# Two more feature blocks of an FFN as block products, another group of features first behind attention, and V of the last chunk computed later

## The chip, the cores and the metric

The kernel runs on one core of a Trainium2 chip. The metric is the device time of one execution in microseconds, the median of several runs. All times below are of single executions or of such medians.

## The reference, cut to what matters

x has 2048 rows of width 640. The result mixes, row by row with a gate, a causal attention with a compressive memory (32 heads of width 20, four chunks of 512 rows) and a gated feed-forward network (FFN) with 1728 features:

```python
g = sigmoid((x * gate_w).sum(-1, keepdims=True))
# attention: q, k, v = x @ wq, x @ wk, x @ wv; for each chunk s of 4:
    logits = q_s @ k_s.T * scale + mask;  a_dot = softmax(logits) @ v_s
    num = phi(q_s) @ M;  den = phi(q_s) @ z + 1e-6;  a_mem = num / den
    o_s = gb * a_mem + (1 - gb) * a_dot        # gb = sigmoid(beta), one per head
    M, z = M + phi(k_s).T @ v_s, z + phi(k_s).sum()
a = o @ wo
# FFN
b = (silu(x @ w1) * (x @ w3)) @ w2
out = g * a + (1 - g) * b
```

All products are of float32 accuracy: both factors are split into a high and a low part, and a product is made of three passes (high x high, high x low, low x high).

## The kernel before, in words

**Tiles.** x comes transposed, five tiles of 128 x 512 for each chunk of 512 rows (`X`, high and low). The 1728 features are 13 blocks of 128 (0 to 12) and half a block of 64, which is called 13. The chunks go in two pairs, A = (0, 1) and B = (2, 3). A feature block of one chunk is made by `ffn_up`: `proj` for the gate (`g`, 15 products of 512 columns: five tiles, three passes) and for the up projection (`u`, 15 products); then ACT and DVE make silu times up and split it into `ht` (high by a cast on ACT, low by a subtraction on POOL). `ffn_down` multiplies a group of three blocks with five column blocks of w2 and adds the result to `acc`: for a group with `lead`, feature block by feature block into five banks at once (30 products for two blocks of features, 45 for three); otherwise column block by column block.

**Block products.** `ffn_unit` makes a feature block pair (gate and up of one feature block, for both chunks of a pair) in another way: `unit` works with seven products of sums of blocks (named a, w, x, y here; a is `f_ff` in the trace), with sums of X that `build_sums` makes once for a pair, and sums of weights that `w_split` makes for each unit on DVE. In pair B, `build_sums(B)` needs the buffers that attention holds, so units of B stand behind attention.

**Weights.** Each weight tile of 128 x 640 is loaded into one of two raw buffers (`wr`, `NRAW`), split by a cast and a subtraction on POOL (L223, L228) into one of six tiles `W` (`NW`), and used by TensorE in order. `w_step` at each step of the dense work loads and splits ahead; `w_get` forces it.

**Attention.** Heads go in quads, 32 quads in all, forty slots each. Two visits a quad: a long one at slot 5 (`s` of the quad, `t` and `o` of the ones before) and a short one at slot 17 (the rest of `s`, and one `t`). `s` are the logits for the row maxima (DVE), `max_rows` turns the maxima and writes them by two small DMAs on ACT's queue into two rows of the tile `qk`; `t` then gives the transposed logits less the maximum, ACT the exponential `P`, `o` the product with v. `load_pair` loads q and k of two heads from DRAM into `qk` by two DMAs.

**What sets the order.** TensorE's order is the program's own (written by hand): a `head`, then attention's slots with dense work between them, then a `tail`. The dense work of attention is a list of segments `segs`, each with the slot at which it has to be done and a list of jobs; a credit in us hands it out evenly over the slots of the segment. `braid(a, b, every, at=...)` puts steps of b between the steps of a. The other engines' order comes from a scheduler, which sorts the instructions by a modelled time; `here` and `behind` pin some of them. `GROUPS` says which feature blocks make one down projection; `LATE` is one such group.

**The places of the change.** Before, GROUPS of B are [0,1,2], [3,4,5], [6,7,8], [9,10,13] (LATE), [11,12]. V of chunks 2 and 3 is computed in the second segment one behind the other (`job_v(B)`), with one loading of the five V weights; features 0 and 1 of B stand in the third. Chunk 3's V isn't kept in SBUF for the memory; its parts go through `ht` buffers (six, `NHT`) and are stored to DRAM. The gate's exponent comes out of V's products, and `gate_turn(3)` transposes it, in K's first block. The tail is half block 13, the loads of the gate's shares, the down projection of [9,10,13] with the sums of X between its steps, unit 11 with the first part of the output projection of chunk 3 between, the output projection, unit 12, and the last down projection.

## Time and profile before

| | |
|---|---|
| median of three runs | 1089.4 us (1089.33 to 1090.75) |
| profiled execution, its own time | 1089.61 us |
| its span in the profile | 1087.9 us |
| TensorE (PE) | 1080.8 us busy, 99%, 6230 products |
| weight loads of TensorE (PEld) | 841.9 us, 77% |
| VectorE (DVE) | 706.9 us, 65% |
| GpSimd (POOL) | 612.8 us, 56% |
| ScalarE (ACT) | 407.0 us, 37% |
| granted TensorE clock | 1.0 of full speed |

A row of a group gives line, engine, operation, output and inputs without their numbers, shapes and a count; after the bar the busy us, the mean ns of one, and the idle us of the engine just before, with what ended most of it. A row of a timeline gives start us, duration us, engine, line and operation, and in brackets what the engine waited for. "f32" products of 512 columns here have overlapping durations, so a price comes from the distance of starts, not from durations. POOLq and ACTq are the queues on which those engines issue DMAs. Lines are those of the kernel before; in the changed kernel they are a few higher.

### The profile page before, as it was taken

Reading aid. Unit: us, or ns where it says so; the run is one execution under the profiler, and the core shown is the slowest. Engines: PE = TensorE matmul, PEld = TensorE weight load, DVE = VectorE, ACT = ScalarE, POOL = GpSimd, SP = SyncE. Lnnn points to the kernel's source line nnn. Section 1 sums busy time; section 2 is a strip of 40 time slices with the busy share of each in tenths; the row PEclk is TensorE's granted clock in tenths of the full one; section 3 lists DMA queues with packets and bytes.
Section 4 is the critical chain, followed back from the end, with each engine's and each line's share of the span. In section 5 each row is a group of like instructions: output and inputs, shape, how many; then the busy total and the mean of one; then the engine's idle time right before and its main releaser. Section 6 shows DMA issues by size and latency. Waiting matters only on the chain.

```text
span 1087.9 us, 18072 instructions
## 1 busy us (share of the span) xinstructions
PE 1080.8 (99%) x6230; PEld 841.9 (77%) x6230; DVE 706.9 (65%) x1867; ACT 407.0 (37%) x874; POOL 612.8 (56%) x751
## 2 busy tenths in 40 slices
PE   9999999999999999999999999999999999999998
PEld 7988878777777777778977777777777777777787
DVE  6477782756765658785344678875557775554996
ACT  6355322233332432245354543424333332242321
POOL 3089674646563664475366447655674664656382
PEclk9999999999999999999999999999999999999999
DMA  9557420553543554555377966455654433435212
GB/s 330 195 179 267 166 61 25 122 111 106 144 114 79 132 135 120 149 155 162 112 242 247 297 218 182 102 159 144 157 143 112 114 102 97 108 93 171 78 47 110
DMA packets 89450, 157.39 MB, mean 145 GB/s; under 512 B 11888, under 2 KB 26128, under 8 KB 89360
## 3 DMA queue, kind: packets, MB, share of 16 engines
q1 hardware_dynamic: 63904, 106.76, 30.8%
q0 software_dynamic: 21424, 42.42, 17.0%
q10 hardware_dynamic: 4032, 7.08, 1.9%
q8 instruction: 49, 0.80, 0.3%
q14 instruction: 41, 0.34, 0.1%
HBM read 100.76 MB, written 54.54 MB: 143 GB/s over the span
## 4 chain that ended last, share of the span: by engine, by line
PE 97%; DMA 1%; ACT 1%; DVE 1%; issue 0%; SPq 0%; DVEq 0%; ACTq 0%
PE f L868 15%; PE g L319 14%; PE u L319 13%; PE v L450 7%; PE op L1125 7%; PE o L970 7%; PE s L914 5%; PE t L949 4%; PE q L319 3%; PE k L319 3%; PE f L854 2%; PE x_ff L554 2%; PE y_ff L554 2%; PE f_ff L554 2%; PE nd L417 2%; PE pm L710 1%
## 5 line engine op out<-in xcount | busy, mean ns | idle before, releaser
L921 DVE CUSTOM_DVE_ANT_0 junk<-s,mask 128x256 bf16<-128x256 f32 (+3 forms) x512 | 249.9, 488 | 86.1 <-PE s L914 53.9
L955 ACT ACTIVATE P<-t 128x512 f32<-128x512 f32 (+1 forms) x384 | 172.0, 538 | 166.8 <-PE t L949 117.3
L228 POOL TENSOR_TENSOR W<-wr,W 128x640 fp32r<-128x640 f32 (+2 forms) x118 | 187.0, 1589 | 19.1 <-ACT W L223 16.8
L960 POOL TENSOR_SCALAR_AFFINE_SELECT P<-P 128x256 f32<-128x256 f32 x192 | 93.6, 497 | 181.0 <-ACT P L955 180.8
L868 PE MATMUL f<-ht,W 128*128 128x512 f32 (+1 forms) x689 | 165.6, 396 | 0.3 <-ACT P L955 0.3
L319 PE MATMUL g<-X,W 128*128 128x512 f32 x660 | 165.0, 398 | 0.3 <-ACT P L955 0.3
L319 PE MATMUL u<-X,W 128*128 128x512 f32 x600 | 152.6, 400 | 0.0
L223 POOL CAST W<-wr 128x640 fp32r<-128x640 f32 (+2 forms) x114 | 86.7, 765 | 116.4 <-PE v L450 34.0
L868 PEld LDWEIGHTS f<-ht,W 128*128 128x128 f32 x689 | 127.4, 188 | 31.1 <-ACT P L955 0.5
L319 PEld LDWEIGHTS g<-X,W 128*128 128x128 f32 x660 | 122.3, 188 | 29.1 <-issue 0.4
L319 PEld LDWEIGHTS u<-X,W 128*128 128x128 f32 x600 | 110.2, 188 | 26.9 <-issue 0.6
L118 POOL TENSOR_TENSOR ht<-ft,ht 128x512 fp32r<-128x512 f32 x40 | 52.1, 1302 | 79.7 <-ACT ht L117 79.5
L891 POOL DMA_DIRECT2D qk<-qkd x128 | 83.4, 653 | 0.3 <-PE s L914 0.2
L914 PE MATMUL s<-qk 60*128 60x256 f32 (+3 forms) x512 | 78.4, 347 | 0.2 <-DVE oq L974 0.2
L970 PE MATMUL o<-P,vg 128*32 128x512 f32 (+3 forms) x1024 | 75.5, 435 | 0.0
L450 PE MATMUL v<-W,X 128*128 128x320 f32 (+1 forms) x480 | 72.4, 311 | 0.0
L450 PEld LDWEIGHTS v<-W,X 128*128 128x128 f32 x480 | 71.2, 189 | 0.8 <-DVE X L145 0.3
L914 PEld LDWEIGHTS s<-qk 60*128 60x128 f32 x512 | 46.6, 185 | 24.2 <-issue 18.5
L970 PEld LDWEIGHTS o<-P,vg 128*32 128x32 f32 x1024 | 30.4, 109 | 41.3 <-issue 31.8
L949 PE MATMUL t<-qk 62*128 62x256 f32 (+3 forms) x512 | 61.8, 320 | 0.4 <-ACT ft L795 0.3
L837 DVE TENSOR_TENSOR acc<-f,acc 128x512 f32<-128x512 f32 x65 | 44.1, 686 | 21.0 <-PE f L868 20.7
L949 PEld LDWEIGHTS t<-qk 62*128 62x128 f32 x512 | 46.2, 186 | 13.0 <-issue 6.9
(310 smaller groups left out, 1604.0 us busy)
## 6 DMA issues: line engine op xcount, KB each, us to landing
qk<-qkd POOLq DMA_DIRECT2D x128, 240.0 KB, 4.1
wr<-in_w_dram SPq DMA_DIRECT2D x69, 320.0 KB
qkd<-qs SPq DMA_DIRECT2D x20, 512.0 KB
qkd<-ks SPq DMA_DIRECT2D x20, 512.0 KB
od<-oq SPq DMA_DIRECT2D x32, 256.0 KB
wr<-in_wo_dram SPq DMA_DIRECT2D x20, 320.0 KB
vg<-vd SPq DMA_DIRECT2D x16, 336.0 KB
xr<-in_xT_dram SPq DMA_DIRECT2D x20, 256.0 KB
```

The source lines that it names most:

```text
L223: hi = (nc.scalar.copy if act else nc.gpsimd.tensor_copy)(w[:, 0, :n], src)
L228: last["low"] = nc.gpsimd.tensor_sub(w[:, 1, :n], src, w[:, 0, :n].bitcast(F32))
L319: nc.tensor.matmul(ps, w[:, a, kb * P:(kb + 1) * P], x[:, b, kb, :], start=n == 0, stop=n == 14)
L450: nc.tensor.matmul(ps[:, :n1 - n0], x[:, a, kb, lb * P:(lb + 1) * P], wvt[kb][:, b, n0:n1], start=n == 0, stop=n == 14)
L868: nc.tensor.matmul(ps[:, :n1 - n0], w, h, start=n == 0, stop=n == len(ms) - 1)
L891: here(nc.gpsimd.dma_start(t[64 * i:64 * i + RH], qkd[c][RH * (h + i):RH * (h + i + 1)]))
L914: nc.tensor.matmul(ps[i][:, o:o + w], q[:, qb * P:(qb + 1) * P], key[:, :w], start=n == 0, stop=n == len(todo) - 1, skip_group_check=True)
L921: r = nc.vector.tensor_tensor_reduce(out=junk[:, :w], in0=ps[i][:, o:o + w], in1=mask[:, L - w:], scale=1.0, scalar=-3.0e38, op0=ALU.add, ...
L949: nc.tensor.matmul(ps[i][:, o:o + L - kb * P], key[:, kb * P:(kb + 1) * P], q[:, kb * P:], start=n == 0, stop=n == len(todo) - 1, skip_gro ...
L955: last["exp"] = nc.scalar.activation(pairs[2 * m + k]["P"][:, i, o:o + n], ps[i][:, b:b + n], AF.Exp, scale=SCALE)
L960: nc.gpsimd.affine_select(d, d, pattern=[[0, 2], [0, n], [1, P]], base=0, channel_multiplier=-1, compare_op=ALU.is_ge, fill=0.0)
L970: nc.tensor.matmul(ps[32 * i:32 * i + 32, kb * P:], heads[2 * p + i]["v"][:, kb], pairs[p + i // 2]["P"][:, i % 2, o:o + n], start=kb == 0 ...
```

## The change

Pair B's groups become [0,1,2], [3,4,5], [6,7,8] (LATE), [13,9,10], [11,12]. Blocks 9 and 10 of B are made by `ffn_unit`, in the tail, as 11 and 12 are. The tail opens with the down projection of [6,7,8], with the sums of X between its steps; then the loads of the shares, half block 13, unit 9 with the first part of the output projection, the output projection, unit 10, the down projection of [13,9,10], units 11 and 12, and the last down projection. V of chunk 3 is moved to the end of the third segment, behind features 0 and 1 of B; for that the V weights are loaded and split a second time. The split of chunk 3's X goes between V of chunk 2 (`XV`), `gate_turn(3)` into feature 2 (`last_gate`). Block 5 of B moves to the fifth segment. The ends of three segments, counted in heads of ten slots, are later by 0.5 (`E2`), 4 (`E3`) and 1 (`E4`). The steps between which the output projections' first parts stand are other ones (`O0A`, `O1A`, `O2A`), as are those of the sums (`TB`). `load_pair` issues the loads of q and k on SP's queue (`SYQ`), and the scale of chunk 3's attention rows comes 12 slots or steps later (`SC`). `ACTSEG` is empty and does nothing.

```diff
-NU, LATE, TB, OB = 1, [9, 10, 13], (1, 6, 9, 12, 15, 18, 21, 23, 25, 27, 29, 31), (1, 3, 5, 7, 9)
+E2, E3, E4, XV, SYQ = 0.5, 15, 2, 5, True
+ACTSEG, SC, O0A, O1A, O2A = (), 26, (12, 14, 17, 19, 21), (2, 6, 10, 13, 16), (6, 13, 20, 27, 34)
+NU, LATE, TB, OB = 1, [6, 7, 8], (1, 2, 4, 6, 8, 9, 14, 17, 20, 23, 26, 28), (1, 3, 5, 7, 9)
...
+    def last_gate():
+        gate_turn(NSEG - 1)
+        yield 100.0
...
-            if n == 2 and mb == 0:
+            if n == 2 and mb == 0 and c < NSEG - 1:
                 gate_turn(c)
...
-              B: [[0, 1, 2], [3, 4, 5], [6, 7, 8], LATE]}
+              B: [[0, 1, 2], [3, 4, 5], LATE, [13, 9, 10]]}
...
-            shares_in = c != 1 and j in GROUPS[A if c < 2 else B][-1]
+            shares_in = c == 0 and j in GROUPS[A][-1] or c > 1 and j == NF
...
-        lead = (cs, js) in ((A, GROUPS[A][0]), (B, GROUPS[B][3]), (B, GROUPS[B][4]))
+        lead = (cs, js) in ((A, GROUPS[A][0]), *((B, js) for js in GROUPS[B][2:]))
...
-            turns = (KB if cs == B else 3) if lead and (c == order[0] or js == GROUPS[B][3]) else 0
+            turns = (KB if cs == B else 3) if lead and (c == order[0] or js == LATE) else 0
...
-            here(nc.gpsimd.dma_start(t[64 * i:64 * i + RH], qkd[c][RH * (h + i):RH * (h + i + 1)]))
+            here((nc.sync if SYQ else nc.gpsimd).dma_start(t[64 * i:64 * i + RH].bitcast(F32 if SYQ else FR), qkd[c][RH * (h + i):RH * (h + i + 1)]))
...
-        after((14, 22, 22, 14)[c], o_scale, c, er)
+        after((14, 22, 22, SC)[c], o_scale, c, er)
...
-    seg += [braid(chain([braid(d, (0, x2), 5)] + q), (0, x3), 4, 10)] + job_v(B)
+    seg += [braid(d, (0, x2), 5)] + q + [braid(chain(job_v(B[:1])), (0, x3), XV)]
     kb_, turns, writes = jobs_k(B)
-    seg += kb_ + turns[:1] + job_q(B[1:], 0, {3: slot}) + turns[1:] + writes
-    segs.append((2 * H - 1.2, seg))
+    seg += kb_ + turns + [braid(job_q(B[1:], 0, {3: slot})[0], writes[0], 3)]
+    segs.append((2 * H - 1.2 + E2, seg))
...
-    segs.append((2 * H + 11, seg))
+    seg += job_v(B[1:])
+    segs.append((2 * H + E3, seg))
...
-    seg = [braid(up[2], o1, 3, at=(2, 5, 8, 12, 15)), braid(o2, job_read(3), 3, 1), job_down(B, 0), braid(chain(jobs_up(B, 1)), (0, load_memory(2)), 5)]
-    segs.append((3 * H + LAG + 1, seg))
+    seg = [braid(braid(up[2], (0, last_gate()), 2), o1, 3, at=O1A), braid(o2, job_read(3), 3, 1), job_down(B, 0), braid(chain([job_up(B, j) for j in GROUPS[B][1][:2]]), (0, load_memory(2)), 5)]
+    segs.append((3 * H + LAG + E4, seg))
+    s2 = [job_up(B, GROUPS[B][1][2])]
     d = job_down(B, 1)
-    u = [job_up(B, j) for j in GROUPS[B][2][:2]]
+    u = [job_up(B, j) for j in LATE[:2]]
     o1, o2 = jobs_oproj(2)
-    seg = [d, braid(chain(u), o1, 5, at=(5, 12, 19, 26, 33)), o2] + [job_up(B, j) for j in GROUPS[B][2][2:]]
-    seg += [job_down(B, 2), braid(chain([job_up(B, j) for j in LATE if j < NF]), (0, load_memory(3)), 5)]
+    seg = s2 + [d, braid(chain(u), o1, 5, at=O2A), o2, braid(job_up(B, LATE[2]), (0, load_memory(3)), 5)]
     segs.append((NJ + LAG, seg))
-    u, d = job_up(B, NF), job_down(B, 3)
-    t = 0, build_sums(B)
-    e = [job_unit(B, GROUPS[B][4][0])]
+    d = job_down(B, 2)
+    u = job_up(B, NF)
+    e = [job_unit(B, 9)]
     o1, o2 = jobs_oproj(3)
-    e += [job_unit(B, j) for j in GROUPS[B][4][1:]]
-    tail = [braid(chain([u, (0, load_shares(B)), d]), t, 3, at=TB), braid(e[0], o1, 3, at=OB),
+    e += [job_unit(B, 10), job_down(B, 3)] + [job_unit(B, j) for j in GROUPS[B][4]]
+    tail = [braid(d, (0, build_sums(B)), 3, at=TB), (0, load_shares(B)), u, braid(e[0], o1, 3, at=OB),
             braid(o2, (0, shared(2)), 3)] + e[1:] + [job_down(B, 4, B)]
```

TensorE behind attention's last product `o62`, in the kernel before (`u3_10` is the up projection of block 10 of chunk 3, `g2_13` the half block of chunk 2, `f2_9_0_0` the down projection of group [9,10,13] of chunk 2 into its first column block; the number behind `ht2_` is the feature block):

```order
L970 MATMUL o62_10903<-P63_10765,vg1_93 32x128 x2
L319 MATMUL u3_10_10890<-X3_5061,W133_10651 128x512 x6
L319 MATMUL g2_13_10937<-X2_4924,W134_10659 128x512 x15
L319 MATMUL g3_13_10979<-X3_5061,W134_10659 128x512 x15
L854 MATMUL f2_9_0_0_11027<-ht2_9_10673,W135_10678 128x512 x3
L854 MATMUL f2_9_1_0_11028<-ht2_9_10673,W135_10678 128x512 x3
```

The same place in the changed kernel:

```order
L976 MATMUL o62_10625<-P63_10501,vg1_93 32x128 x2
L321 MATMUL u3_8_10609<-X3_5302,W131_10434 128x512 x3
L860 MATMUL f3_6_0_0_10657<-ht3_6_9780,W132_10442 128x512 x3
L860 MATMUL f3_6_1_0_10658<-ht3_6_9780,W132_10442 128x512 x3
L860 MATMUL f3_6_2_0_10659<-ht3_6_9780,W132_10442 128x512 x3
```

The down projection of blocks 9, 10 and 13 has given its place to that of 6, 7 and 8 of chunk 3; half block 13 stood two rows ahead of the projection that uses it (third, behind 9 and 10, in rows that follow); ahead of the new one stands the end of up 8, whose `ht3_8` it uses third.

TensorE from the end of the short visit (`s22_4`) to the long one that follows (`s23_0`), in the kernel before:

```order
L914 MATMUL s22_4_0_8349<-qk0_90 128x128
L914 MATMUL s22_4_1_8350<-qk0_90 128x128
L868 MATMUL f3_0_3_0_8318<-ht3_2_7561,W106_7946 128x512 x3
L868 MATMUL f3_0_4_0_8378<-ht3_0_7092,W104_7657 128x512 x3
L868 MATMUL f3_0_4_0_8378<-ht3_1_7282,W105_7938 128x512 x3
L868 MATMUL f3_0_4_0_8378<-ht3_2_7561,W106_7946 128x512 x3
L319 MATMUL g2_3_8391<-X2_4924,W107_7967 128x512 x15
L319 MATMUL u2_3_8429<-X2_4924,W108_7978 128x512 x15
L914 MATMUL s23_0_0_8448<-qk1_91 128x512
L914 MATMUL s23_0_1_8449<-qk1_91 128x512
```

The same in the changed kernel (ahead of these rows stand `s22_4` and one row more of `f2_0_2_0`):

```order
L874 MATMUL f2_0_2_0_8327<-ht2_1_6993,W110_8104 128x512 x3
L874 MATMUL f2_0_2_0_8327<-ht2_2_7572,W111_8112 128x512 x3
L874 MATMUL f2_0_3_0_8338<-ht2_0_6692,W109_7822 128x512 x3
L874 MATMUL f2_0_3_0_8338<-ht2_1_6993,W110_8104 128x512 x3
L874 MATMUL f2_0_3_0_8338<-ht2_2_7572,W111_8112 128x512 x3
L874 MATMUL f2_0_4_0_8349<-ht2_0_6692,W109_7822 128x512 x3
L874 MATMUL f2_0_4_0_8349<-ht2_1_6993,W110_8104 128x512 x3
L874 MATMUL f2_0_4_0_8349<-ht2_2_7572,W111_8112 128x512 x3
L874 MATMUL f3_0_0_0_8361<-ht3_0_6932,W109_7822 128x512 x3
L874 MATMUL f3_0_0_0_8361<-ht3_1_7122,W110_8104 128x512 x3
L874 MATMUL f3_0_0_0_8361<-ht3_2_7778,W111_8112 128x512 x3
L920 MATMUL s23_0_0_8372<-qk1_91 128x512
```

Where a down projection's last four rows, a gate block and an up block stood, there is now a stretch of the down projection of features 0, 1 and 2.

POOL in the third quarter of the program, kernel before, where the loads of q and k (L891) stand among the masks (AFFINE_SELECT) and the weights (CAST and TENSOR_TENSOR of `W`):

```order
L960 AFFINE_SELECT P46_8719<-P46_8719 128x2x256
L891 DMA qk1_91<-qkd3_71 60x2x512 x2
L228 TENSOR_TENSOR W115_8808<-wr99_8574,W115_8808 128x640
L960 AFFINE_SELECT P47_8756<-P47_8756 128x2x128
L960 AFFINE_SELECT P47_8756<-P47_8756 128x2x256
L891 DMA qk1_91<-qkd3_71 60x2x512 x2
L223 CAST W116_8881<-wr100_8650 128x640
```

SP's queue in the changed kernel, about the same place (`wr` are weight loads, `od2` a store of attention's rows, `oall2` loads of them):

```order
L897 DMA qk0_90<-qkd3_71 60x2x512 x2
L189 DMA wr101_8570<-in_w13_dram 128x640
L189 DMA wr102_8578<-in_w2_dram 128x640
L982 DMA od2_78<-oq44_8662 128x512
L897 DMA qk1_91<-qkd3_71 60x2x512 x2
L189 DMA wr103_8597<-in_w2_dram 128x640
```

The loads of q and k (now L897) have left POOL and stand on SP between the loads of weights, the stores and the loads of attention's rows.

More of the change, by code (lines that the diff above doesn't have):

```diff
@@ L221, in w_split @@
         else:
-            act = "tail" in last and kind in ACTHI
+            act = "tail" in last and kind in ACTHI or len(segs) in ACTSEG and "exp" in last
             hi = (nc.scalar.copy if act else nc.gpsimd.tensor_copy)(w[:, 0, :n], src)
@@ L1209, in gated_mix @@
     o1, o2 = jobs_oproj(0)
-    seg = [braid(d, o1, 3, at=(13, 15, 17, 19, 20)), (0, load_shares(A[:1])), o2]
+    seg = [braid(d, o1, 3, at=O0A), (0, load_shares(A[:1])), o2]
     u0, u1 = jobs_up_by_chunk(A, 4)
```

## The prediction

> **What bounds the kernel now.** I read the page's busy table and clock first, then the chain that ended last, a table of windows by stage, and the timeline where a stage is not full.
>
> ```profile
> span 1087.9 us, 18072 instructions
> PE 1080.8 (99%) x6230; PEld 841.9 (77%) x6230; DVE 706.9 (65%) x1867; ACT 407.0 (37%) x874; POOL 612.8 (56%) x751
> PEclk9999999999999999999999999999999999999999
> PE 97%; DMA 1%; ACT 1%; DVE 1%; issue 0%; SPq 0%; DVEq 0%; ACTq 0%
> ```
>
> TensorE is busy for 99% of the span at the full clock, and the chain is 97% TensorE. No other engine is above 65%. So the time is the sum of TensorE's products, and a change pays by fewer products or by less idle time between them. Where the idle time lies shows in windows (us, PE busy, weight loads, DVE, ACT, POOL, clock, DMA):
>
> ```profile
> 204.00:455.00 251.00, 250.82 (x1469) 188.04 (x1468) 164.83 (x526) 77.56 (x176) 138.77 (x175) 1.00 0.46 117
> 455.00:488.00 33.00, 32.26 (x178) 24.73 (x178) 26.86 (x63) 18.33 (x36) 21.52 (x24) 1.00 0.58 161
> 488.00:523.00 35.00, 34.72 (x241) 30.61 (x239) 15.66 (x51) 15.79 (x38) 15.34 (x25) 1.00 0.49 150
> 523.00:996.00 473.00, 473.00 (x2949) 359.40 (x2951) 297.18 (x930) 186.04 (x413) 276.82 (x360) 1.00 0.56 157
> 996.00:1022.00 26.00, 25.44 (x122) 20.06 (x115) 18.66 (x33) 8.78 (x16) 8.58 (x9) 1.00 0.31 95
> 1022.00:1088.00 66.00, 62.71 (x286) 49.80 (x284) 54.53 (x74) 12.39 (x21) 37.07 (x27) 1.00 0.24 80
> ```
>
> Between 204 and 1022 us only 0.18 + 0.74 + 0.28 + 0.56 = 1.76 us are idle. The rest of the page's 7.1 us lies at the start and behind the last product, where this change does nothing. So waits can give back 1.6 us at most (the last three); the gain has to come from the count of products, while new waits have no such limit.
>
> **The price of a product**, in the stretch behind attention:
>
> ```profile
> 996.51 1.66 PE L319 MATMUL u<-X,W 128*128 128x512 f32 x6
> 998.01 7.17 PE L319 MATMUL g<-X,W 128*128 128x512 f32 x30
> 1005.01 7.17 PE L854 MATMUL f<-ht,W 128*128 128x512 f32 x30
> 1012.74 11.89 PE L854 MATMUL f<-ht,W 128*128 128x512 f32 x50 [0.56 <-DVE ht L798]
> ```
>
> 30 products start at 998.01 and the next group at 1005.01: 7.00 / 30 = 0.233 us for each 512 columns. The Trainium skill (TensorE: Matmul & The Clock Gate, Back-to-back issue gap) gives some 131 ns in a sustained stream and 216 for an isolated one; by these the first term below would be an estimated 1.6 or 2.6 us. The trace does not agree, it has 233, and the sum goes by that.
>
> **Part 1, the block products: -2.8 us.** Feature blocks 9 and 10 of chunks 2 and 3 cost 60 products each before (two chunks, gate and up, 15 each). As a unit of seven block products the built program issues 15 + 6 + 18 + 15 = 54 (products a, w, x, y). All of TensorE's list goes from 5586 to 5574 instructions; every other kind is only moved. 12 x 0.233 = 2.8 us, all on the path. The cover for what a unit asks of others: on DVE some 20 more operations and on POOL 9 more weight subtractions and 3 more casts, against 4 fewer `ht` subtractions, and 128 loads taken off POOL:
>
> ```profile
> L228 POOL TENSOR_TENSOR W<-wr,W 128x640 fp32r<-128x640 f32 (+2 forms) x118 | 187.0, 1589 | 19.1 <-ACT W L223 16.8
> L223 POOL CAST W<-wr 128x640 fp32r<-128x640 f32 (+2 forms) x114 | 86.7, 765 | 116.4 <-PE v L450 34.0
> L118 POOL TENSOR_TENSOR ht<-ft,ht 128x512 fp32r<-128x512 f32 x40 | 52.1, 1302 | 79.7 <-ACT ht L117 79.5
> L891 POOL DMA_DIRECT2D qk<-qkd x128 | 83.4, 653 | 0.3 <-PE s L914 0.2
> ```
>
> 9 x 1.59 + 3 x 0.77 - 4 x 1.30 = 11.4 us more, 83.4 less: POOL ends lighter by 72 us.
>
> **Part 2, the first down projection of the tail: -0.6 us.** Before, half block 13 is made at 998 and used by the down projection that follows it at once; TensorE waits 0.56 us for its `ht` (last row above). Now the tail opens with the down projection of 6, 7, 8, and 13 is followed by unit 9, the output projection and unit 10 before its own use. What could be late instead is `ht` 8 of chunk 3: its last product stands right in front, but the down projection goes block by block and needs it after 30 products, 7.0 us. The copy, cast and subtraction behind that product take 0.68, 0.62 and 1.30 us (the two rows below and the `ht` group above), and POOL may be busy with a cast and subtraction of a weight, up to 3 us: 5.6 us. The durations behind the last product:
>
> ```profile
> 998.53 0.68 DVE L788 SCALAR_TENSOR_TENSOR ft<-fu,u 128x512 f32<-128x512 f32 x1
> 999.25 0.62 ACT L117 CAST ht<-ft 128x512 fp32r<-128x512 f32 x1 [1.44 <-DVE ft L788]
> ```
>
> So 7.0 less 5.6 leaves 1.4 us. I take no wait there, with up to 0.5 us of loss, and -0.6 for the one that goes.
>
> **Part 3, V of chunk 3 moved: 0.** Its 120 products are issued later, none more. The five V weights are loaded and split a second time: 5 loads and 5 x (0.77 + 1.59) = 11.8 us of POOL (part of the counts above), under 14 us of features 0 and 1, and under POOL's freed time. The copies of V take two buffers in turn, since four of six hold `ht` of features 0 and 1; the third copy waits for the store of the first, one block after it was issued. V's products go at
>
> ```profile
> 20.24 35.55 PE v L450 x240
> ```
>
> 0.148 us, a block of 30 in 4.4 us. No row gives that store's time; the nearest of like size is the load of q and k (KB each, median us to landing),
>
> ```profile
> qk<-qkd POOLq DMA_DIRECT2D x128, 240.0 KB, 4.1
> ```
>
> less than a block. I take 0, bounds 0 and +1. Moving it and the split of chunk 3's X out of 455 to 523 thins the stretches with 0.74 and 0.28 us of idle time. Those are waits for PSUM banks that ACT and DVE free late while they also split X; the split still stands there, spread wider. I take half, -0.5, bounds 0 and -1.0.
>
> **Part 4, denser visits: +0.7.** Gate and up of features 9 and 10 (120 products) and the down projection of 6, 7, 8 (90) leave the attention stretch: 210 x 0.233 = 49 us less to put between attention's visits (TensorE's products for one quad of heads, a long and a short one each). The step with a deadline is from a short visit to the next long one: maxima on DVE, a turn through ACT and DVE, two small loads on ACT's queue, then `t`. The tightest case before:
>
> ```profile
> 760.34 0.51 PE L914 MATMUL s<-qk 60*128 60x256 f32 x4
> 761.30 3.04 PE L868 MATMUL f<-ht,W 128*128 128x512 f32 x12
> 764.18 3.68 PE L319 MATMUL g<-X,W 128*128 128x512 f32 x15
> 767.70 3.63 PE L319 MATMUL u<-X,W 128*128 128x512 f32 x15
> 771.26 0.50 PE L914 MATMUL s<-qk 60*128 60x512 f32 x2
> 771.60 0.57 PE L949 MATMUL t<-qk 62*128 62x512 f32 x4
> 766.47 1.07 ACTq L937 DMA_DIRECT2D qk<-mr x2
> ```
>
> Short visit at 760.34, loads issued by 767.54 (7.2 us), first `t` at 771.60 without a wait: the landing takes at most 4.1 us. There 42 products lay between; in the new order 36, 39, 39 and 36 plus a turned block lie in the four shortest. 36 x 0.233 + 0.96 + 0.34 = 9.7 us leaves 2.5 us for the landing. Bounds: nothing if it lands in 2.5; 1.6 + 0.9 + 0.9 + 0.3 = 3.7 us if it takes all of 4.1. I take 0.7, near the lower end: the upper one is only how long that load could have taken.
>
> **Part 5, unit 12 right behind unit 11: 0.** A unit's second weight tile is loaded once the one before has been split. From unit 11's start: its last split 2.0, a cast 0.8, issue and landing
>
> ```profile
> wr<-in_w_dram POOLq DMA_DIRECT2D x4, 320.0 KB, 3.3
> 1007.38 0.42 DVE L213 TENSOR_TENSOR ws<-wr 128x256 f32<-128x256 f32 x1
> 1009.29 0.43 DVE L216 TENSOR_TENSOR wr<-wr 128x256 f32<-128x256 f32 x1
> 1009.75 0.73 ACT L223 CAST W<-wr 128x640 fp32r<-128x640 f32 x1 [0.21 <-DVE wr L216]
> 1010.56 1.57 POOL L228 TENSOR_TENSOR W<-wr,W 128x640 fp32r<-128x640 f32 x1 [7.05 <-ACT W L223]
> 1012.10 1.72 POOL L228 TENSOR_TENSOR W<-ws,W 128x512 fp32r<-128x512 f32 x1
> ```
>
> 3.9, sums 2.0 (five operations, first and last shown) with 1.4 of others between, 0.7, 1.6: 12.4 us. It is needed after 54 + 6 products, 14.0 us. Margin 1.6; I take 0, bounds 0 and +1.5.
>
> **Part 6, the q and k loads on SP's queue: 0.** Each waits until TensorE has left the tile, and behind it on SP stand weight loads and stores. The places without slack are those where five weights are wanted at once, as before the first output projection:
>
> ```profile
> 430.50 1.41 POOL L223 CAST W<-wr 128x640 fp32r<-128x640 f32 x2 [0.19 <-PE f L868]
> 431.87 3.54 POOL L228 TENSOR_TENSOR W<-wr,W 128x640 fp32r<-128x640 f32 x2
> 435.38 0.62 PE L1125 MATMUL op<-oT,W 128*128 128x512 f32 x2
> ```
>
> The last weight is ready at 435.41 and used at once, but what its cast waited for was TensorE, not a load. I take 0: the loads behind are of tiles wanted many products later.
>
> **Sum.** -2.8 - 0.6 - 0.5 + 0.7 = -3.2 us. The profiled execution took 1089.61 us for its span of 1087.9; it lies 0.2 over the median of 1089.4, which I start from: **1086.2 us**, a span near 1084.7.
>
> **The rivals.**
> First, the visits eat the gain: the landing takes its bound in all four gaps (+3.7 in place of +0.7) and the time is 1089.2, no change. For it: 2.5 us is less than any gap of before left. Against it: from 523 to 996, where 30 visits lie, TensorE has no idle time at all (473.00 of 473.00 above).
> Second, and slower: SP's queue becomes the bound of the weights. These loads took 4.1 us to land from POOL (row in part 3); a weight load behind them is late by up to that. Five bursts of five weights (two V, three output projections in attention) give 5 x 4.1 = 20 us at most; with half of it, 10 us, the sum is 1096. It turns the sign from 0.7 us a burst, and passes +0.2% from 1.1 us. Against it: `wr` is loaded a tile or more ahead outside the bursts. The Trainium skill (DMA: Bandwidth & Descriptors, Queues, rings and completion order) speaks for this rival: SP has one row of rings, consumed in ring order, while another issuer's row is served in turn with it. The trace of before, where these loads are POOL's, cannot show it.
> Third, no other waits at all and both idle stretches gone: -2.8 - 0.6 - 1.0, 1085.0.
>
> **How the numbers follow.** Forecast 0.52, third rival 0.12, first 0.22, second 0.14. The measurement tells 0.2%, 2.2 us, from no change: below 1087.2 is faster, above 1091.6 slower. Forecast and third rival are faster save for 0.06 of the forecast's spread; the first rival is the same; of the second 0.02 stay within. Faster 0.58, same 0.30, slower 0.12. The range goes from 1084.0 (the third rival and one us for idle time that the modelled ends of products may hide) to 1091.3 (the first, 1089.2, with the upper bounds of part 2, 1.1 above its value, and of part 3, 1.0), and leaves out most of the second.
>
> **What would show it.** 12 fewer products at 0.233 us; no wait for `ht` behind the half block; idle time of TensorE between 455 and 523 under 0.6 us; long visits at 4.5 us, or longer ones with a wait for the small loads if the first rival holds; waits for `W` at the start of V or of the output projections if the second does. A pitch off 0.233, or a wait of a kind that no row above has, would make the forecast wrong.

## The result: 10 us slower, and the profile after

The changed kernel takes 1099.62 us (median of six runs) against 1089.75 for the kernel before on the same chip; the ratio is 1.0093 (95% interval 1.0081 to 1.0104). The forecast was 1086.2. The profiled execution took 1099.54 us with a span of 1097.8, 9.9 us more than before. The six executions lie between 1098.22 and 1102.79 us, so a difference of 1 us between this kernel and a variant of it is not resolved. The busy table and the clock of the changed kernel:

```profile
span 1097.8 us, 18076 instructions
PE 1082.4 (99%) x6218; PEld 839.3 (76%) x6218; DVE 725.2 (66%) x1897; ACT 412.4 (38%) x884; POOL 546.0 (50%) x635
PEclk9999999999999999999999999999999999999999
```

TensorE has 12 products less (6230 to 6218) at the same clock, and POOL is lighter by 67 us (72 forecast); still the span has grown. By stage (us, PE busy, weight loads, DVE, ACT, POOL, clock, DMA):

```profile
455.00:488.00 33.00, 32.79 (x193) 24.83 (x186) 25.38 (x68) 19.04 (x40) 22.52 (x24) 1.00 0.57 166
488.00:523.00 35.00, 35.00 (x240) 30.15 (x239) 20.09 (x60) 16.21 (x37) 13.57 (x19) 1.00 0.51 169
523.00:955.00 432.00, 427.20 (x2721) 322.66 (x2720) 279.18 (x896) 178.50 (x400) 209.45 (x268) 1.00 0.54 163
955.00:1036.00 81.00, 77.42 (x337) 59.66 (x336) 66.62 (x92) 19.53 (x34) 57.82 (x50) 1.00 0.34 102
1036.00:1097.00 61.00, 57.23 (x249) 45.27 (x247) 43.46 (x64) 11.44 (x20) 19.48 (x17) 1.00 0.21 71
```

From 455 to 523 the idle time has fallen from 1.02 us to 0.21. From 523 to the end of attention, where nothing was idle before, 4.8 us are now, and in the tail up to 1036 us another 3.6. What TensorE waited for, in the trace's table of waits (us in total, times, longest):

```profile
PE t L955 <- DVE m L927: 1.7, 2, 1.0
PE ge L473 <- ACT ns L145: 1.5, 2, 0.9
PE op L1131 <- DVE oall L1061: 1.5, 2, 1.4
PE f L860 <- ACT ht L119: 1.5, 2, 0.8
PE f L860 <- DVE acc L843: 1.4, 1, 1.4
PE o L976 <- DVE ft L794: 1.0, 1, 1.0
PE op L1131 <- POOL W L230: 0.5, 1, 0.5
PE f L860 <- POOL ht L120: 0.3, 1, 0.3
PE y_ff L560 <- DVE on L1059: 0.3, 1, 0.3
```

Before, the whole table past the start came to some 1.7 us. Almost every new row names DVE, or ACT behind DVE.

Ends of products are modelled, so starts tell more. I call a gap what the distance from one TensorE instruction's start to the next has beyond the instruction's own time, where that is over 0.1 us; the own time is taken as 0.453 ns for each column (232 ns for 512). The table below adds the gaps of each stage, in us of the span. The usual small gaps of attention are in it, and products at a lowered clock; distances behind `o` are left out; so columns are to be compared with the first row. Attention ends at 996 us before, at 955 in the changed kernel, so the last column of before holds some of it. Gaps and clock (the mean granted clock) are those of the one profiled execution, "time" is the median of all in us, and each row's kernel is told below. One of e12's five executions took 1306 us at a granted clock of 0.75, and e12's time is the median of the other four.

| kernel | time | clock | 0-420 | 420-523 | 523-700 | 700-955 | 955-end |
|---|---|---|---|---|---|---|---|
| before | 1089.4 to 1090.2 | 1.000 | 11.6 | 5.1 | 4.8 | 7.7 | 2.0 |
| changed | 1099.62 | 1.000 | 12.3 | 4.1 | 6.8 | 12.8 | 7.5 |
| e1 q, k on POOL | 1108.58 | 0.995 | 11.5 | 6.2 | 11.5 | 12.4 | 11.5 |
| e2 before, q, k on SP | 1093.31 | 0.999 | 12.4 | 5.3 | 4.6 | 8.8 | 3.6 |
| e3 before, new tail | 1109.62 | 0.994 | 11.4 | 5.1 | 4.8 | 21.4 | 6.8 |
| e4 V back | 1114.08 | 0.997 | 11.1 | 5.9 | 6.1 | 20.6 | 9.4 |
| e5 gates later | 1100.03 | 1.000 | 11.5 | 4.5 | 6.5 | 13.5 | 6.8 |
| e6 unit 10 first | 1101.06 | 0.996 | 12.4 | 4.1 | 6.6 | 13.8 | 8.5 |
| e7 later segments | 1113.91 | 0.993 | 11.5 | 4.1 | 8.1 | 21.7 | 10.6 |
| e8 ht on POOL | 1103.18 | 0.997 | 12.2 | 4.5 | 6.7 | 12.7 | 11.8 |
| e9 9, 10 direct | 1097.09 | 1.000 | 12.8 | 4.1 | 6.5 | 12.8 | 1.4 |
| e10 e3 + padding | 1119.86 | 0.997 | 12.0 | 5.0 | 4.9 | 14.8 | 6.6 |
| e11 before, V moved | 1108.22 | 0.992 | 11.5 | 11.0 | 11.6 | 13.7 | 1.5 |
| e12 old tail | 1095.04 | 1.000 | 11.2 | 4.3 | 7.0 | 9.3 | 2.7 |
| e13 e12, q, k on POOL | 1101.24 | 0.997 | 11.6 | 6.2 | 12.7 | 9.8 | 1.3 |
| e14 e11, q, k on SP | 1095.38 | 1.000 | 12.3 | 6.6 | 7.3 | 10.1 | 1.3 |
| e15 three units | 1099.91 | 0.998 | 12.6 | 5.3 | 4.8 | 10.0 | 10.4 |
| e16 W's low on DVE | 1099.74 | 0.996 | 11.9 | 4.3 | 7.1 | 12.2 | 10.2 |

For the changed kernel the sums are 43.5 against 31.2: 12.3 us of new waits, less 2.8 us for the products, 9.5 of the measured 9.9. Of the 12.3, 5.5 are the tail's, 5.1 lie from 700 to 955, 2.0 from 523 to 700, 0.7 at the start, and 420 to 523 gave back 1.0. Single gaps over 0.25 us make most of it. From 700 to 955 `t` of two long visits waits 1.3 and 0.3 us where the small loads are late (799, 896), and two products wait 0.8 and 1.2 us for PSUM banks that DVE frees late (705, 897). In the tail the largest are 1.6 us (969), 1.5 (1005), 1.0 (1083) and 0.8 (1040), all on results of DVE or of ACT behind it.

### The profile page after: what moved, and what is told of

Read it like the earlier page. It is cut to its first block, busy times and chain, and to the rows that moved or that the text cites. A ratio compares the mean times of both kernels' runs of the same rounds, so it can differ in the third digit from the quotient of the medians.

```text
span 1097.8 us, 18076 instructions
## 1 busy us (share of the span) xinstructions
PE 1082.4 (99%) x6218; PEld 839.3 (76%) x6218; DVE 725.2 (66%) x1897; ACT 412.4 (38%) x884; POOL 546.0 (50%) x635
## 5 line engine op out<-in xcount | busy, mean ns | idle before, releaser
L230 POOL TENSOR_TENSOR W<-wr,W 128x640 fp32r<-128x640 f32 (+2 forms) x125 | 197.9, 1586 | 32.4 <-ACT W L225 29.3
L225 POOL CAST W<-wr 128x640 fp32r<-128x640 f32 (+2 forms) x117 | 89.3, 768 | 176.6 <-PE v L452 42.1
L874 PE MATMUL f<-ht,W 128*128 128x512 f32 (+1 forms) x639 | 153.8, 396 | 0.2 <-ACT P L961 0.2
L321 PE MATMUL g<-X,W 128*128 128x512 f32 x600 | 151.5, 400 | 0.0
L874 PEld LDWEIGHTS f<-ht,W 128*128 128x128 f32 x639 | 118.0, 188 | 29.0 <-issue 0.5
L321 PE MATMUL u<-X,W 128*128 128x512 f32 x540 | 136.4, 399 | 0.0
L321 PEld LDWEIGHTS g<-X,W 128*128 128x128 f32 x600 | 110.3, 188 | 26.0
L321 PEld LDWEIGHTS u<-X,W 128*128 128x128 f32 x540 | 99.7, 188 | 24.3 <-issue 0.6
L120 POOL TENSOR_TENSOR ht<-ft,ht 128x512 fp32r<-128x512 f32 x36 | 46.4, 1290 | 70.8 <-ACT ht L119 70.6
L843 DVE TENSOR_TENSOR acc<-f,acc 128x512 f32<-128x512 f32 x65 | 44.0, 686 | 23.3 <-PE f L874 23.0
L860 PE MATMUL f<-ht,W 128*128 128x512 f32 x187 | 46.1, 399 | 3.2 <-ACT ht L119 1.5
```

The lines of the kernel that those rows point to most:

```text
L225: hi = (nc.scalar.copy if act else nc.gpsimd.tensor_copy)(w[:, 0, :n], src)
L230: last["low"] = nc.gpsimd.tensor_sub(w[:, 1, :n], src, w[:, 0, :n].bitcast(F32))
L321: nc.tensor.matmul(ps, w[:, a, kb * P:(kb + 1) * P], x[:, b, kb, :], start=n == 0, stop=n == 14)
L860: nc.tensor.matmul(ps, w2s[n][:, b, fb * P:(fb + 1) * P], hts[c, j][:, a], start=n == i == 0, stop=n == len(js) - 1 and i == len(ab) - 1)
L874: nc.tensor.matmul(ps[:, :n1 - n0], w, h, start=n == 0, stop=n == len(ms) - 1)
```

## The experiments

**One part alone, one part undone (e1 to e4).**

e1: `SYQ` is False in the changed kernel, so that q and k are loaded from POOL again.

> The changed kernel with one part undone: q and k are loaded from POOL's queue again. The theory, that the loss has three places (tail, visits, gate turns), gives this part only the wait in the long visit at 799 us, 1.3 us, where the second small load behind the maxima was issued 3.1 us after the first: 1098.3, and the tail from 955 us on unchanged within 0.5 us. The rival, that SP's queue is late with everything behind these loads, wants at least half of the 9.9 us back: under 1095. If POOL's freed time carried the rest, the run is slower than the changed kernel.

1108.58, ratio to before 1.0170 (1.0156 to 1.0185): 9 us slower than the changed kernel, the third of the three cases. The queue's change, costed at nothing, carries other parts of the change. By starts, the waits for the gate's turns grew to 2.1 and 3.1 us (0.8 and 1.1 in the changed kernel), and at the second one DVE shows why; DVE's row, and the two of POOL beside it:

```profile
689.38 2.63 DVE L466 SCALAR_TENSOR_TENSOR gate<-gate 128x4 f32<-128x4 f32 x1
689.12 1.31 POOL L897 DMA_DIRECT2D qk<-qkd  x2
690.44 1.54 POOL L230 TENSOR_TENSOR W<-wr,W 128x640 fp32r<-128x640 f32 x1
```

An operation on 128 x 4 numbers, which takes 0.16 us in the changed kernel (686.28), took 2.63 and ended when POOL's subtraction did (691.98). e16 returns to this.

e2: the kernel before, q and k loaded by `nc.sync`.

> The kernel before with this part alone: q and k loaded from SP's queue. The theory: the visits of before have 42 products and more between short and long one, so a late small load is covered; 1089.4 to 1090.5. The rival of SP's queue: 1094 or more. If lighter POOL is worth something by itself: under 1089.

1093.31 (1.0028, 1.0019 to 1.0036), between the two expectations and nearer to the rival's: 1.6 us of new waits behind 955, 1.1 from 700 to 955, 0.8 at the start. By itself the queue is a loss of 3 us, not of 10.

e3: the kernel before with the changed kernel's groups, last segment and tail.

> The kernel before with the tail and the groups of the changed kernel alone (units 9 and 10, down projection of 6, 7, 8 first); V of chunk 3, the queue of q and k and the early segments as before. The theory: 12 products less give -2.8 us, DVE late in the tail +5.8, denser visits in the last two chunks +1 to +3: 1093 to 1096, with the waits for DVE in the tail as in the changed kernel. The rival, that the moved V or the queue makes the loss and the units pay: 1086 to 1087.

1109.62 (1.0176, 1.0162 to 1.0190), worse than every theory had it. The tail's new waits are 4.8 us, near the expected 5.8. The rest lies at the visits, in one row of the table of waits, and in the clock, from 860 to 900 us:

```profile
PE t L949 <- DMA qk<-mr: 9.9, 5, 2.9
860.00:900.00 40.00, 34.45 (x217) 22.66 (x214) 27.08 (x83) 16.11 (x36) 22.19 (x29) 0.91 0.38 100
```

Five long visits wait for the two small loads of maxima, up to 2.9 us each. By the program's order the work from the start of a short visit to the next long one is here down to 7.1, 7.9, 9.2, 9.9 and 10.0 us (products at 0.2325 us); before, none was under 10.4. And behind the waits the granted clock falls.

e4: the changed kernel with V of chunk 3, its gate turn and two segment ends where they were.

> The changed kernel with V of chunk 3 back behind V of chunk 2, its gate turn in K's first block, and the segment ends of before. The theory: the two waits for the gate's turn go (1.0 us at 525, 1.1 us at 687), the waits at 455 to 502 come back (0.9 us), and one weight loading less: 1098 to 1099. The rival, that the moved V crowds the visits behind it and makes the larger part of the loss: under 1095.

1114.08 (1.0224, 1.0210 to 1.0238), 14.5 us slower. The moved V, with its tables, is a gain inside the changed kernel. I read it so: its 120 products fill the visits which the lost 210 products leave thin. Without them the least work between a short visit and its long one is 7.9 us, and the gaps from 700 to 955 grow by 7.8. That does not explain all of it: the longest wait, 4.5 us at 802, stands behind 39 products, as many as visits of the changed kernel have without a wait, and its small loads took 7 us from issue to landing.

**Where the changed kernel's own waits come from (e5 to e8).**

e5:

```diff
-if n == 2 and mb == 0 and c < NSEG - 1:
+if n == 2 and mb == (1 if c == 2 else 0) and c < NSEG - 1:
-braid(up[2], (0, last_gate()), 2)
+braid(up[2], (0, last_gate()), 10)
```

> The changed kernel with the two gate turns later: chunk 2's in K's second block (30 products later), chunk 3's ten steps into feature block 2 (in place of two). The theory that TensorE waits there only because DVE hasn't made the gate yet: no wait at the turns, -1.0 and -1.1 us, 1097.5. The rival, that DVE is simply behind at these places and TensorE would wait for its next result instead: 1099 to 1100 with the wait on another row.

1100.03, as the rival had it, though 0.4 us from the changed kernel is within the scatter; the trace tells more than the time. No wait is left at the turns; instead K's transpose waits 1.1 us for DVE at 530, and a bank held by DVE's maxima 2.0 us at 702. DVE is behind at these places, and TensorE waits for the next result that it asks for.

e6: `job_unit(B, 10)` is put ahead of the output projection's second part, with its weights.

> The changed kernel with unit 10 ahead of the output projection of chunk 3, in place of behind it. The theory that DVE, full with unit 9 and the normalized rows at once, is late for the output projection (1.8 us at 1005) and that unit 10 has no cover for its ht (0.8 us at 1040): both waits go, -2.6 us, 1097. The rival, that DVE's work in the tail as a whole is too much for TensorE's: the waits move into unit 10, and the time stays within 1 us of the changed kernel's 1099.6.

1101.06. Both waits went, and one of 2.9 us came inside unit 9, for a bank that the normalized rows hold (2.7 us by the table of waits, on DVE's L1059). Again the wait moves and the sum stays: the rival. Behind this wait the trace has the granted clock at 0.5 for 6.8 us.

e7: `E3, E4 = 20, 6` in place of 15, 2.

> The changed kernel with the ends of the third and fourth segment later (20 and 6 in place of 15 and 2), so that the last third of attention has more products between its visits: the shortest gap from a short visit to the long one behind it has 10.0 us of work in place of 9.3, and all gaps together fall short of 11.4 us by 3.5 in place of 6.9. The theory that visits wait where there is too little between them: the waits between 695 and 935 fall from 4 us to 2 or less, 1097 to 1098. The rival, that these waits come of DVE's load by the normalized rows and of the queue: no change, 1099 to 1100.5.

1113.91, a miss by both. The shortest gaps were longer, and the time 14 us worse. One long wait is of another kind, for the loads of q and k that stand on SP behind weight loads (table of waits, then windows of the clock):

```profile
PE s L920 <- DMA qk<-qkd: 5.5, 2, 5.0
772.00:776.00 4.00, 1.64 (x7) 1.19 (x9) 0.77 (x3) 0.00 (x0) 0.00 (x0) 0.53 0.86 248
776.00:780.00 4.00, 4.00 (x16) 3.11 (x15) 2.36 (x10) 1.21 (x4) 0.64 (x1) 0.61 0.47 119
```

So the second rival of the prediction, SP's queue, does exist, in another order than the changed kernel's. The run says nothing clean about the gaps, since the moved work changed the loads too.

e8: the low part of `ht` of units 9 and 10 on POOL.

> The changed kernel with the low part of ht of units 9 and 10 made by POOL in place of DVE (4 operations: 2.7 us off DVE, 5.2 us on POOL). The theory that DVE bounds the tail: the waits at 1005 and 1040 shrink by 0.5 to 1.5 us together, 1098 to 1099. The rival that POOL's weight splitting bounds the tail: slower by 1 us or more, with waits for W.

1103.18, the rival: 1005 shrank by 0.5 us and 1040 went, but the unit's second weight was late on POOL and TensorE waited 2.5 us for `W` (`w_ff`, L225) and 0.7 more. So these four operations found no free place on POOL either, although POOL is busy for only 54% of the changed kernel's tail.

**Which step made it (e9 to e12).**

e9: `job_up` in place of `job_unit` for 9 and 10, at the same places of the tail.

> The changed kernel with blocks 9 and 10 at their places in the tail, but made directly (60 products each) and not as units. The theory that the two units load DVE and POOL in the tail more than TensorE's 12 products are worth: +2.8 us for products, -4 to -5 us of the 5.8 us of new waits behind 955 us: 1097 to 1098.5. The rival, that the order of the tail makes the waits, whatever the form of 9 and 10: 1102 to 1103.

1097.09 (1.0067, 1.0054 to 1.0079), in the expected range. With 12 products more the kernel is 2.5 us faster: the gaps of the tail fall from 7.5 us to 1.4, and DVE's busy time behind 955 from 110 us to 96. The two units, the core of the change, lose there. Not all of it is DVE's work. The changed kernel's largest gap in the tail, 1.6 us at 969, is a wait for an addition to `acc` on DVE. That stands behind sums of X for the units, and the first of these waits on DVE for its own load from DRAM. Its row in the changed kernel, then in e9, where the load landed 3.7 us earlier and TensorE has no wait there:

```profile
966.31 0.69 DVE L528 TENSOR_TENSOR unit<-unit 128x512 f32<-128x512 f32 x1 [8.14 <-DMA unit<-in_xT_dram]
962.55 0.69 DVE L528 TENSOR_TENSOR unit<-unit 128x512 f32<-128x512 f32 x1 [2.37 <-DMA unit<-in_xT_dram]
```

e10: e3 with the gate products of 6, 7, 8 made twice (the copy is overwritten).

> The kernel of e3_tail_alone with 90 products (21 us) added that nobody reads: the gate product of blocks 6, 7 and 8 of chunks 2 and 3 is made twice, in the last segment of attention. The theory that visits wait there for want of products between them: of 13.9 us of waits from 800 to 955 us about 12 go, and the lowered clock behind them (0.91 from 860 to 900 us, some 3 us) too, so the 21 us cost 6 to 9: 1116 to 1119. The rival, that these waits come from the loads or DVE whatever lies between: 1128 to 1131.

1119.86: 21 us of added work cost 10.2. Half of it was free: the gaps from 700 to 955 fell by 6.6 us, and another 3.8 us went from the distances behind `o`, which the table leaves out. That is nearer to the theory than to the rival, with less given back than it said: waits of 1.9 us at 956 and of some 2 us around 887 stayed, the latter with a lowered clock behind it:

```profile
887.00:893.00 6.00, 5.10 (x19) 3.81 (x18) 4.35 (x18) 1.59 (x3) 2.74 (x5) 0.72 0.83 165
```

e11: the kernel before with V moved (its gate turn, X's split and the ends of two segments with it).

> The kernel before with V of chunk 3 moved alone (with the split of its X, its gate turn and the ends of the second and third segment). The theory: two waits for the gate's turns (+2.1 us) against thinner stretches from 455 to 523 us (-0.9 us), visits with no less between them than before: 1090.5 to 1092. The rival, that the moved V pays by itself since the later visits get more between them: under 1089. If it were a loss of its own: over 1095.

1108.22 (1.0166, 1.0151 to 1.0182): 18 us where I expected 1 or 2. The old steps of the output projection no longer fit (5.9 us of new gaps at 420 to 445), and:

```profile
PE ge L471 <- ACT ns L143: 4.2, 2, 2.2
PE f L872 <- POOL W L228: 4.0, 1, 4.0
```

e12: the changed kernel with the old groups, last segment and tail.

> The changed kernel with the groups, the last segment's work and the tail of before: what is left of the change is V, the queue of q and k, block 5's place and the tables. The theory that thinner visits and the tail make the loss: 1090 to 1094, the shortest late gaps being those of before or longer. The rival that V and the queue make it: 1097 or more.

1095.04 (1.0047, 1.0033 to 1.0061). That is above the theory's 1094 and below the rival's 1097. So tail and thinner visits make 4.6 us of the loss net (7.4 and the products' gain of 2.8), V with the queue and the tables some 5. By the gaps of the profiled executions the split is 9.0 of 12.3 and 3.3; e12's profiled execution, 1093.53, was its fastest.

**What carries the moved V, and why DVE's operations are long (e13 to e16).**

e13: e12 with `SYQ` False. e14: e11 with q and k on SP.

> The kernel of e12_old_tail with the loads of q and k on POOL. The theory that the moved V (weights split a second time on POOL, gate turns right behind V) is borne only by the POOL time that the queue's change frees: 1100 to 1105, with later gate turns (2 us and more each) and a wait for W at the first output projection. The rival, that the tables of steps (O0A, O1A, O2A) and block 5 make the difference between 1108.2 of V alone and 1095.8, and the queue is a loss of 3 us as it is on the kernel before: 1092 to 1093.

> The kernel of e11_v_alone (V moved, all other tables as before) with q and k on SP's queue. The theory that freed POOL time carries V: the wait of 4.0 us for W at 752 and half of the gate turns' 4.5 us go, 1098 to 1102, the cluster of waits at 432 to 441 (5 us), which the old table of steps makes, stays. The rival, that the tables do it all: 1106 to 1111.

1101.24 and 1095.38, the theory's side both times (e14 3 us better than it said). For e14:

```profile
PE ge L471 <- ACT ns L143: 2.1, 2, 1.5
PE f L872 <- POOL W L228: 1.6, 1, 1.6
```

The queue's change takes 13 us off V's 18 in the old order (e11, e14), 9 us in the changed kernel (e1) and 6 in e12's order (e13). Part of the rest is the old table: the gaps from 420 to 523 are 6.6 us in e14 and 4.3 in e12.

e15: the kernel before with `LATE = [9, 13]`, so that 10 becomes a third unit.

> The kernel before with one block more as a unit in the tail in place of two: the group [9, 10, 13] becomes [9, 13], and block 10 joins 11 and 12 (three units, a last down projection of three blocks); V, queue and tables as before. Products: 6 less, -1.4 us. The theory that each unit brings 8 us of DVE work into the tail and takes 60 products from the visits: shortest gap 9.9 us in place of 10.4, waits of 1 to 3 us in the tail and up to 1 at the visits: 1089 to 1092. The rival, that the loss begins only with the fourth unit, where DVE is 90% busy: 1088 to 1088.8, faster than before.

1099.91 (1.0089, 1.0076 to 1.0102), worse than both. Its largest new wait is 2.8 us for the half block's `ht`, which now has one block of the down projection ahead of it where two stood. So the run doesn't tell what a third unit alone would cost; it shows only that this version doesn't pay either. No run here beats the kernel before.

e16: the low part of the tail's weights by `nc.vector` in place of `nc.gpsimd`, in the changed kernel.

> The changed kernel with the low parts of the tail's 28 weight tiles made on DVE in place of POOL (44.5 us off POOL, 28 x 0.7 to 0.85 = 20 to 24 us on DVE). The theory that DVE's operations with two inputs from SBUF stand while a POOL operation that reads SBUF runs (in the tail of the changed kernel 1.2 to 1.8 us in place of 0.68 where POOL is busy): they go back to 0.68 to 0.8 on average, which gives back 15 to 20 us of DVE, so DVE's busy time behind 955 us stays within 8 us of its 110 in spite of the 28 added operations; the time 1097 to 1102. The rival, that these operations are long of themselves (their form, or ACT's accesses): means of 0.94 to 1.35 us stay, DVE's busy time grows by 20 us or more, and the time is 1105 or more.

1099.74, no change of time, and the theory's durations in three groups. DVE's operations in the tail of the changed kernel, L670, L668 and L1061 with two inputs from SBUF, L843 with one from PSUM (busy, mean ns):

```profile
L670 DVE SCALAR_TENSOR_TENSOR fu<-fu,unit 128x512 f32<-128x512 f32 x8 | 10.6, 1353 | 0.0
L668 DVE TENSOR_TENSOR fu<-fu,sh 128x512 f32<-128x512 f32 x8 | 8.6, 1078 | 0.1
L1061 DVE TENSOR_TENSOR oall<-on,gm 128x512 fp32r<-128x512 f32 x5 | 5.8, 1165 | 0.0
L843 DVE TENSOR_TENSOR acc<-f,acc 128x512 f32<-128x512 f32 x20 | 13.1, 682 | 4.8 <-PE f L874 4.7
```

The same in e16, where POOL has only three weight subtractions left behind 955 us, all before 971:

```profile
L670 DVE SCALAR_TENSOR_TENSOR fu<-fu,unit 128x512 f32<-128x512 f32 x8 | 6.3, 799 | 0.0
L668 DVE TENSOR_TENSOR fu<-fu,sh 128x512 f32<-128x512 f32 x8 | 5.5, 681 | 0.0
L1061 DVE TENSOR_TENSOR oall<-on,gm 128x512 fp32r<-128x512 f32 x5 | 3.5, 696 | 0.0
L843 DVE TENSOR_TENSOR acc<-f,acc 128x512 f32<-128x512 f32 x20 | 13.2, 681 | 4.1 <-PE f L874 4.1
```

25 of the 28 subtractions fall behind 955 us and cost DVE 19 us there (its own groups of L230: 14.4, 2.7 and 2.2), and its busy time behind 955 us grew by 3 only, from 110.1 to 113.3: what POOL's work had held up made up for the rest. Other operations with two SBUF inputs stayed long on average (L811 0.99 us, `ht<-fu,ht` 0.96); the long ones among them are those that still ran beside an operation of POOL with two inputs. The form is not the reason: in the changed kernel's whole trace `ht<-fu,ht` takes 0.69 us in the ten cases with no POOL instruction beside it, and 1.36 on average in the six beside an operation of POOL with two inputs. TensorE then waited 3.5 us in one place (968) and 2.2 in another (1007) in place of several smaller ones, and behind each the granted clock was 0.5 for 3.4 us.

## Why the prediction was wrong, point by point

**The count of products (part 1, -2.8) held.** The trace has 12 fewer (6230 and 6218), and the pitch, the distance from start to start, is the same; the chain of the changed kernel has

```profile
1045.10 9.30 PE f L874 x40
```

9.30 / 40 = 0.2325 us.

**The cover of the units (part 1's second half, "20 more operations on DVE") is the step that failed most, in the tail.** The prediction counted these operations over the whole kernel, where DVE is 65% busy, gave them no price, and put their effect at nothing. The trace has 30 more (1897 for 1867) and 18.3 us more of DVE. e9 prices the two units as they stand in this order: their form costs 6.1 us of gaps in the tail against 2.8 of products, and 1.6 of the 6.1 hang on the late load shown under e9. The sums in SBUF also grew dearer: the groups `fu<-fu,unit` and `fu<-fu,sh` took 1.35 and 1.08 us on average beside POOL's subtractions, 0.78 and 0.70 in the tail of before.

It is tempting to say that DVE is too full in this tail, but the busy share does not show it. A stretch of 70 us in the tail of before, and one in the changed kernel's:

```profile
1008.00:1078.00 70.00, 69.44 (x310) 54.85 (x308) 63.74 (x89) 18.22 (x31) 40.52 (x29) 1.00 0.19 59
975.00:1045.00 70.00, 67.54 (x296) 51.99 (x295) 63.12 (x87) 16.91 (x29) 45.48 (x35) 1.00 0.20 58
```

DVE is busy for 91% and 90% of these stretches, and TensorE is idle for 0.56 and 2.46 us. What differs is which of DVE's results TensorE wants while DVE is behind: now the additions to `acc` (969), the normalized rows for the output projection (1005) and `ht` of unit 10 (1040). That reading follows from the rows; no run moves the results and leaves the work as it is.

**Part 2 held half.** The wait for the half block's `ht` (0.56) is gone, and the one for `ht` 8 came at 0.3 in the table of waits, inside its bound of 0.5. A row that I hadn't looked for came behind it: 1.4 us for `acc`, whose additions stand on DVE behind the sums of X and their load.

**Part 3 saw the gain and missed the cost.** The thinner stretch gave 0.8 us (I had 0.5). But before, V of chunk 3 stood between V of chunk 2 and the turn of its gate, and a block of K ahead of chunk 3's turn. Now both turns follow their V closely and wait 0.8 and 1.1 us, and e5 shows DVE late there: with the turns later, TensorE waits for other results of DVE. And I called the second splitting of V's weights hidden under POOL's freed time: that is right, but then part 6 wasn't free. It was V's cover (e11, e14).

**Part 4 looked for the wait at the wrong visits, and took too little.** I took 0.7 of 0 to 3.7, all from the four shortest gaps, with the landing as the thing that could be late; the gaps from 700 to 955 grew by 5.1. In the trace three of these four visits (short ones at 749, 848 and 924) have no wait, and the fourth (885) has 0.3. The two loads of the tightest case before were done 1.7 us after their issue, by the trace's records of semaphores, and so are most others: the lower end was right there. The wait came at a visit with 51 products in between. ACT's two loads, TensorE's visit, and ACT's next operation:

```profile
793.31 3.65 ACTq L943 DMA_DIRECT2D qk<-mr  x2
799.30 0.50 PE L920 MATMUL s<-qk 60*128 60x512 f32 x2
800.84 0.74 PE L955 MATMUL t<-qk 62*128 62x512 f32 x6 [1.03 <-DVE m L927]
797.01 0.62 ACT L119 CAST ht<-ft 128x512 fp32r<-128x512 f32 x1 [4.81 <-DMA oall<-od]
```

The short visit was at 786.3. The first load was issued 7.0 us later, but was done only at 799.66, 6.3 us after its issue. The second was issued at 796.45 (10.1 us after the visit), since ACT's queue stood until a load of attention's rows (`oall`, issued on SP at 786.81) was done at 796.43; it was done at 800.70. The row names DVE, whose maximum ended at 800.71, so this trace alone does not tell the two apart. In e1 the same visit waits 1.6 us and its row names the loads, done 6.8 and 7.0 us after their issue; there q and k come from POOL, so their move to SP's queue is not needed for this wait. The other late waits there (0.8 at 705, 1.2 at 897) are banks that DVE frees late while it normalizes rows. An order with still fewer products does wait at its short gaps (e3), and products added there take much of that away (e10). Nor did I see that the moved V was the answer to it: I costed it at zero where its return costs 14.5.

**Part 5 held:** no wait for `W` inside unit 12 in the changed kernel.

**Part 6**, taken as 0, is +3.1 us alone (e2) and -9 with the rest (e1); its range should have come from who needs POOL, not only from who stands behind on SP.

**The rivals.** The first was the nearest in kind, but its four gaps were not where the visits lost: at most 1.6 of their 5.1 us are waits for the small loads, and it lacked the tail. The second has its mechanism in e7; in the changed kernel no wait of TensorE is put down to the loads of q and k. None of mine had late results of DVE, and those are the larger part.

Open: what part of e12's remaining 5 us is each table's; why some small loads take 4 to 7 us to land; and what a third unit costs when the half block keeps its cover.

## What to carry to other kernels

An edit that saves the bound engine's work by adding to others is to be costed in the stage where the work lands, result by result: for each thing that the bound engine asks for there, list what now stands ahead of it on the other engine, and what that waits for in turn. A busy share doesn't replace the list; here DVE was 90% busy with and without the waits. When work is taken out of a stage that it covered, list each chain that ran beneath it with its own length and variation, and expect several small waits rather than one. Parts that look free may be each other's cover: price them in pairs.

## What the runs showed of the hardware

- A DVE operation with two SBUF inputs is held up by POOL's subtractions: the means fell from 1353 to 799 ns, 1078 to 681 and 1165 to 696 when these went (e16); one with a PSUM input kept 682 and 681. The Trainium skill (SBUF — State Buffer, SBUF: two separate sides) has it as an exclusive lock on a port pair that the two engines share; the traces agree. By that rule the units' sums in SBUF were to be priced up, and the prediction did not.
- Waits of TensorE lower the granted clock behind them: 0.91 from 860 to 900 us in e3, 0.53 and 0.61 for 8 us behind the wait of 5 us in e7, 0.72 in e10 behind some 2 us in several pieces; in the profiled execution of the changed kernel, with no single wait over 1.6 us, it stayed at 1.00. The traces' clock records show it as stretches at 0.5 of 3.4 or 6.8 us. Over the 18 profiled executions here, all 18 waits of 2.16 to 5.22 us (by starts) have such a stretch beginning within 1.5 us of their end; of 15 waits from 1.73 to 2.10 us two have one. In them a product of 512 columns takes 0.427 us in place of 0.2325 (e16, 1010.18 to 1010.61), so by my estimate from these numbers such a stretch costs some 1.5 or 3.1 us on top of the wait. The Trainium skill (TensorE: Matmul & The Clock Gate, Why this matters for your kernels) warns of gaps above some 3 us; e3's waits, 2.9 us at most by the table of waits, and the one of 2.2 us in e16 already did it.
